# First batch of an attention and feed-forward kernel: float32 kept through the second mixing and the product with v

## Chip, cores and metric

The kernel runs on one core of one Trainium2 chip. The metric is the device time of one execution in microseconds (us). The engines are named as in the profile: PE (matmul), PEld (its weight loads), DVE (vector), ACT (scalar, activation), POOL (GpSimd), SP (the queue that issues the transfers). Each engine works through its own queue in order.

## What is computed

Four batches, 12 heads, 448 rows, head size 64, all float32 inputs. The attention mixes the 12 heads twice, once before and once after the softmax; the result goes through a feed-forward network of width 2048 with a gate.

```python
scores = scale * np.matmul(q, k.transpose(0, 1, 3, 2))
scores = np.einsum('bhij,hg->bgij', scores, w_pre)
scores = scores - np.max(scores, axis=-1, keepdims=True)
attn = np.exp(scores)
attn = attn / (np.sum(attn, axis=-1, keepdims=True) + 1e-09)
attn = np.einsum('bhij,hg->bgij', attn, w_post)
out = np.matmul(attn, v)
# then, with x = out as (1792, 768):
h = x @ w_in
g = h * (1.0 / (1.0 + np.exp(-1.702 * h)))
y = g @ w_out
```

## The kernel before

**Tiling.** A batch's 448 rows are cut into 45 groups of 10 rows (the last has 8). A group with its 12 heads makes 120 partitions, and a mixing over heads is one matmul with a 120x120 matrix that holds the 12x12 weights once for each row. Twelve groups make a chunk of 120 rows; a batch has four chunks. Four batches of 45 groups are 180 steps, and the main loop (L895 to L965) issues the work of one step after the other.

**One group's way.** `gather` (L263) brings the scores of the group from DRAM. `mix` (L273, PE, float32) applies the first mixing. `peak` (L282, DVE) takes the negative maximum, `expo` (L288) the exponential and its sum on ACT, and a small POOL instruction (L297) adds 1e-9 to the sum. `inverse` (L300, DVE) is the reciprocal. Then the weights are normalized and cut into two float16 parts: `weigh` (L304, POOL) and `upper` (L312, ACT) both multiply by the reciprocal, `lower` (L318, POOL) takes the difference. `post` (L326, PE) is the second mixing, transposed: four column blocks of 112, each with three float16 products (upper by upper, upper by lower, lower by upper: L334 to L336). `keep_upper` (L348, ACT) and `keep_lower` (L352, DVE) bring its result out of PSUM, again as two float16 parts. `context` (L358, PE) multiplies them with v, which is also kept as two float16 parts, made for batch 0 by three ACT or POOL instructions (L192, L196) and three DVE instructions (L200). `x_upper` and `x_lower` (L383, L387) take the result out.

**What is issued in a step.** At step i: `gather(i+4)`, `mix(i+1)`, `keep_upper(i-4)`, `weigh`, `upper` and `lower` of group i-1, `peak(i)`, `expo(i)`, then the jobs of the planner, `post(i-3)`, scores and contexts that are due, `keep_lower(i-4)` and, last, `inverse(i)`. PSUM holds two result tiles of the second mixing (`pp`, bufs=2).

**The planner.** `job` and `run_jobs` (L650, L656) hold work that is not tied to a group: the sums of squares and scales of q, k and v, and the conversion of 16 weight blocks from 64-bit to two float16 parts (`convert`, L422), each with 15 DVE instructions for the bits (L442 to L462), 3 for the lower part (L495), 3 sums of squares on ACT (L96) and 3 upper parts on ACT or POOL (L490, L492). Each engine has a budget of tokens (`spend`, `refill`) of 4.3 per step, never above 4.5; a job that isn't urgent waits until its engine has half its cost. `add_all` (L104) sums over partitions with a small matmul (L108) into the last 16 columns of the last `pp` tile, and DVE reads it (L109).

**After the first batch.** When a batch's attention is done, its feed-forward units are put between the steps (`hidden`, `project`, L545 and L584, on PE), 2.15 quanta to a step; after the last step only they remain.

Of the kernel before, what the change touches and what calls it, by code (L numbers as in the profile page):

```python
# [9 lines left out]
F32 = mybir.dt.float32  # L10
# [3 lines left out]
AF = mybir.ActivationFunctionType  # L14
# [8 lines left out]
GI = 10  # L23
# [15 lines left out]
def attention_then_feed_forward(ctx, tc, q, k, v, w_pre, w_post, w_in, w_out, out):  # L39
# [76 lines left out]
    def load(name, b, i, use, tag="op"):  # L116

        t = st[name, b, i] = flow.tile(SH[name], F32, name=f"{name}{use}{i}_{b}", tag=tag, bufs=THIRDS)
        w = t.shape[1]
        nc.sync.dma_start(out=t, in_=SRC[name][b][:, i * w:(i + 1) * w])  # L120

    def load_whole(name, i):

        t = st[name, 0, i] = flow.tile(
            [128, NPAIR // THIRDS, S], F32, name=f"{name}f{i}_0", tag=f"{name}p{i}"
        )
        w = t.shape[1]
        nc.sync.dma_start(out=t, in_=SRC[name][0][:, i * w:(i + 1) * w])

# [17 lines left out]
    def scale(name, b):  # L147

        m = top_of(name, b)
        e = stat.tile([128, 1], F32, name=f"e{name}_{b}", tag="e" + name)  # L150
        s = stat.tile([128, 1], F32, name=f"s_{name}{b}", tag="s" + name)
        root_bits(e, m)
        nc.vector.reciprocal(s, e)
        nc.vector.tensor_scalar_mul(s, s, 2.0 ** -50)
        nc.vector.tensor_scalar_mul(e, e, 2.0 ** 63)
        st["e" + name, b], st["s" + name, b] = e, s
        if name == "v":
            nc.vector.tensor_scalar(
                ex[:, b:b + 1], e, e_wp, 2.0 ** -12, op0=ALU.mult, op1=ALU.mult
            )  # L160

    def mixing(b):
        wa = keep.tile([KG, KG], F32, name=f"wa_{b}", tag="wa", bufs=2)
# [34 lines left out]
    def lower_part(name, b, i, eng="D"):  # L198
        u, l, src, s = pair_of(name, b, i)
        nc.vector.scalar_tensor_tensor(l, src, s, u, op0=ALU.mult, op1=ALU.subtract)  # L200
# [59 lines left out]
    def rows_of(g):  # L260
        return g * GI, min(GI, S - g * GI)
# [26 lines left out]
    def expo(i):  # L288
        K = rows_of(steps[i][1])[1] * H
        e = flow.tile([KG, S], F32, name=f"e_{i}", tag="e", bufs=3)  # L290
        sm = stat.tile([KG, 1], F32, name=f"sm_{i}", tag="sm")
        nc.scalar.activation(  # L292
            e[:K], row.pop(("mx", i))[:K, :S], AF.Exp, bias=row.pop(("nm", i))[:K, 0:1],
            scale=1.0, accum_out=sm[:K, 0:1],
        )
        rs = stat.tile([KG, 1], F32, name=f"rs_{i}", tag="rs")
        nc.gpsimd.tensor_scalar(rs[:K], sm[:K], 1e-9, 2.0 ** -10, op0=ALU.add, op1=ALU.mult)  # L297
        row["e", i], row["rs", i] = e, rs

    def inverse(i):  # L300
        K = rows_of(steps[i][1])[1] * H
        nc.vector.reciprocal(row["rs", i][:K], row["rs", i][:K])  # L302

    def weigh(i):  # L304
        K = rows_of(steps[i][1])[1] * H
# [34 lines left out]
    def mixed_to(i, j):  # L340
# [4 lines left out]
            st["p", b, c, j] = mixed.tile([CP, NR, H, CI], F16, name=f"p{j}_{b}_{c}", tag=f"p{j}")  # L345
        return st["p", b, c, j].rearrange("p r h i -> p (r h) i")[:, :, off:off + n]

    def keep_upper(i):  # L348
        row["p1", i] = mixed_to(i, 1)
        nc.scalar.copy(row["p1", i], row["pp", i])  # L350
# [7 lines left out]
    def context(b, c, pr):  # L358
        i0, n = chunk(b, c)
        if pr % 3 == 0:  # L360
            av = bank(f"av_{b}_{c}_{pr}", "av", 1)
            st["av"] = av[:, :3 * n].rearrange("p (a i) -> p a i", i=n)
        av = st["av"]
        terms = [(jc, i, j) for jc in range(NR) for i, j in ((0, 1), (0, 2), (1, 1))]
        w = H // THIRDS
        for t, (jc, i, j) in enumerate(terms):
            for d in range(2):
                h = 2 * pr + d
                nc.tensor.matmul(  # L369
                    av[d * D:(d + 1) * D, pr % 3, :],  # L370
                    st["vp", b, h // w][:, i, h % w, jc * D:(jc + 1) * D],
                    st["p", b, c, j][:, jc, h, :n],
                    start=(t == 0), stop=(t == len(terms) - 1),
                )
        return av

    def x_of(b):
        if ("x", b) not in st:
            st["x", b] = flow.tile([128, 2, NCC, S], F16, name=f"x_{b}", tag="x", bufs=2)
            st["mx", b] = stat.tile([128, 2 * NCH], F32, name=f"mx_{b}", tag="mxs", bufs=2)  # L380
        return st["x", b]

    def x_upper(b, c, half, av):  # L383
        i0, n = chunk(b, c)
        nc.scalar.activation(x_of(b)[:, 0, 3 * half:3 * half + 3, i0:i0 + n], av, AF.Copy, scale=2.0 ** -15)

    def x_lower(b, c, half, av):  # L387
        i0, n = chunk(b, c)
        x = x_of(b)[:, :, 3 * half:3 * half + 3, i0:i0 + n]
        nc.vector.scalar_tensor_tensor(  # L390
            x[:, 1], av, 2.0 ** -15, x[:, 0], op0=ALU.mult, op1=ALU.subtract
        )

    def x_size(b, c, half):
# [228 lines left out]
    def spend(eng, cost):  # L623
        tokens[eng] -= cost
# [25 lines left out]
    def job(first, eng, cost, f, after=(), stage=None, urgent=False):  # L650
        j = {"urgent": urgent, "first": first, "eng": eng, "cost": cost, "f": f, "stage": stage,
             "after": [a if isinstance(a, tuple) else (a, 1) for a in after]}
        jobs.append(j)
        return j
# [175 lines left out]
    for i in range(AHEAD):  # L830
        gather(i)
    for i in range(THIRDS):
        load("v", 0, i, "a")
    sq = []
    for i in range(THIRDS):
        stage_users["op"].append([])
        sq.append(job(1, {"A": 1.6}, 0, lambda eng, i=i: squares("v", 0, i, eng, 2), urgent=True))
    j = job(1, "D", 0.2, lambda: join("v", 0), after=sq, urgent=True)
    j = job(1, "D", 0.7, lambda: scale("v", 0), after=[j], urgent=True)
    for i in range(THIRDS):  # L840
        up = job(1, {"A": 1.0, "G": 1.6}, 0, lambda eng, i=i: upper_part("v", 0, i, eng), after=[j], urgent=True)
        low = job(1, "D", 1.05, lambda i=i: lower_part("v", 0, i), after=[up], urgent=True)
        stage_users["op"][i] += [sq[i], up, low]


    at_scores = {}
# [48 lines left out]
    while quanta or i < N + LAG + 12:  # L895
        dense = i >= N + LAG
        t_step = 4.3 if not x_done else 5.2
        refill(t_step)
        if i + AHEAD < N:
            b, g = steps[i + AHEAD]  # L900
            assert (b, g // GPC) == (0, 0) or (b, g // GPC, NPAIR - 1) in sent
            gather(i + AHEAD)
        fetch_ahead(i)
        if i + 1 < N:
            mix(i + 1)
        if 0 <= i - LAG - 1 < N:
            keep_upper(i - LAG - 1)
            spend("A", 0.55)
        if 0 <= i - 1 < N:
            weigh(i - 1)  # L910
            spend("G", 0.87)
            upper(i - 1)
            spend("A", 0.6)
            lower(i - 1)
            spend("G", 1.07)
        if i < N:
            peak(i)
            spend("D", 0.62)
            expo(i)
            spend("A", 0.82)  # L920
        run_jobs(i)
        slot()
        if x_done:
            owed += RATE
        if owed >= 1 and do_quantum(i):
            owed -= 1
            slot()
        if 0 <= i - LAG < N:
            post(i - LAG)
        for b, c, pr in at_scores.pop(i, []):  # L930
            while quanta and quanta[0][0] == "h" and quanta[0][3]:
                do_quantum(i)
                owed -= 1
            start(scores_chain(b, c, pr, *scores(b, c, pr)))
        for b, c, pr in at_context.pop(i, []):
            if c == 0 and pr == 0 and b >= 2:
                while h_done.get(NS * (b - 1) - 1, 0) < 6:
                    assert do_quantum(i)
                    slot()
            av = context(b, c, pr)  # L940
            if pr % 3 == 2:
                start(context_chain(b, c, pr, av))
            if c == NCH - 1 and pr == NPAIR - 1:
                z = i
                a = job(z + 2, "D", 0.2, lambda b=b: join_x(b), urgent=True)

                def finish(b=b, z=z):
                    scale_x(b)
                    x_done[b] = cur[0] + 1
                job(z + 3, "D", 0.9, finish, after=[a], urgent=True)  # L950
        slot()
        while owed >= 1 and do_quantum(i):
            owed -= 1
            slot()
        if 0 <= i - LAG - 1 < N:
            keep_lower(i - LAG - 1)
            spend("D", 0.64)
        if i < N:
            inverse(i)
            spend("D", 0.15)  # L960
        owed = min(owed, 3.0)
        if i >= N + LAG + 8:
            owed += 3
        cur = [i + 1]
        i += 1  # L965
# [40 lines left out]
```

## Time and profile before

| what | value |
|---|---|
| median of 3 runs | 1103.3 us (1103.12 to 1106.03) |
| profiled execution | 1107.87 us, of which the span of instructions is 1106.1 us |
| busy share of the span | PE 86%, DVE 63%, ACT 57%, POOL 41% |
| mean granted clock of PE | 0.907 |

The profiled execution is 4.6 us above the median. Its span is cut here at 37 us (first mixing), 251 us (the exponential of group 44, the last of batch 0), 300 us, 500 us and 950 us (last group of batch 3). Busy shares are averages over stages; what ends last in a stage is read from the chain of waits in that stage.

### The profile page before, as it was taken

What the parts mean: (1) busy time and instruction counts of PE and PEld (TensorE: products, weight loads), DVE (VectorE), ACT (ScalarE), POOL (GpSimd) and SP (SyncE); (2) the same over time, 40 slices, a digit from 0 to 9 for tenths busy, and PEclk for the clock granted to TensorE, in tenths of its full rate; (3) what the DMA queues carried; (4) which work ended last, traced back from release to release, by engine and by line L of the source; (5) the groups of instructions that cost most, each with busy time, mean ns of one, the idle gap of its engine ahead of it and who ended that gap; (6) DMA issues with size and microseconds to landing.
All of it is one profiled execution on the core that took longest, in us unless ns stands there. A gap on an engine that the chain in (4) does not pass through costs nothing.

```text
span 1106.1 us, 20863 instructions
## 1 busy us (share of the span) xinstructions
PE 948.5 (86%) x7716; PEld 545.1 (49%) x7716; DVE 699.2 (63%) x1455; ACT 631.3 (57%) x1432; POOL 452.9 (41%) x612
## 2 busy tenths in 40 slices
PE   3577676778688897689979899999999999999998
PEld 1233434445445554346546555565555566555554
DVE  4489777968887859956565357554664556543334
ACT  2466676676666665566565756755655555422332
POOL 0254546645553435545454345434443444210221
PEclk7577868877788899899999999999999999999999
DMA  7776776586576766655476654654654532234332
GB/s 250 212 244 225 264 269 203 158 282 192 178 226 212 242 202 207 208 168 186 130 212 211 204 174 154 204 185 134 205 168 142 179 105 88 75 120 144 114 114 79
DMA packets 67433, 201.00 MB, mean 182 GB/s; under 512 B 7764, under 2 KB 32468, under 8 KB 67332
## 3 DMA queue, kind: packets, MB, share of 16 engines
q1 hardware_dynamic: 66928, 199.59, 56.7%
q8 instruction: 61, 1.00, 0.4%
q14 instruction: 40, 0.33, 0.1%
q10 hardware_dynamic: 404, 0.09, 0.1%
HBM read 143.02 MB, written 56.62 MB: 180 GB/s over the span
## 4 chain that ended last, share of the span: by engine, by line
PE 56%; DVE 26%; ACT 7%; issue 5%; DMA 4%; POOL 1%; SPq 1%; ACTq 0%; DVEq 0%; POOLq 0%
PE po L584 18%; PE h L545 17%; PE mx L278 7%; PE av L369 4%; DVE w_p L495 3%; DVE p L353 3%; PE qk L242 3%; DVE nm L285 2%; DVE w_f L442 2%; PE pp L334 2%; DVE w_f L456 2%; DVE w_f L446 2%; PE pp L335 2%; PE pp L336 2%; DVE w_f L462 2%
## 5 line engine op out<-in xcount | busy, mean ns | idle before, releaser
L321 POOL TENSOR_TENSOR a<-w,a 120x448 f16<-120x448 f32 x180 | 201.2, 1118 | 153.0 <-issue 85.9
L584 PE MATMUL po<-g,wt 128*128 128x448 f16 x1152 | 250.7, 362 | 11.2 <-DVE th L566 7.2
L545 PE MATMUL h<-x,wt 128*128 128x448 f16 x1152 | 245.1, 357 | 3.3 <-ACT pt L608 1.7
L307 POOL TENSOR_SCALAR w<-e,rs 120x448 f32<-120x448 f32 x180 | 122.2, 679 | 306.7 <-DVE rs L302 281.8
L278 PE MATMUL mx<-r,wa 120*120 120x448 f32 x360 | 195.3, 628 | 29.0 <-DMA r<-sd 19.3
L315 ACT ACTIVATE a<-e,rs 120x448 f16<-120x448 f32 x180 | 121.4, 674 | 159.9 <-DVE rs L302 159.8
L334 PE MATMUL pp<-wp,a 120*112 120x120 f16 x720 | 140.0, 232 | 54.9 <-DVE p L353 54.4
L584 PEld LDWEIGHTS <-wt 128*128 128x128 f16 x1152 | 111.0, 100 | 135.3 <-issue 52.9
L545 PEld LDWEIGHTS <-wt 128*128 128x128 f16 x1152 | 109.5, 99 | 114.0 <-issue 28.8
L614 DVE SCALAR_TENSOR_TENSOR acc<-po,ct,acc 128x448 f32<-128x448 f32 x137 | 93.3, 682 | 81.1 <-PE po L584 79.1
L336 PE MATMUL pp<-wp,a 120*112 120x120 f16 x720 | 139.2, 231 | 0.0
L335 PE MATMUL pp<-wp,a 120*112 120x120 f16 x720 | 139.2, 231 | 0.0
L335 PEld LDWEIGHTS <-a 120*112 120x112 f16 x720 | 103.4, 144 | 56.7 <-issue 50.6
L334 PEld LDWEIGHTS <-a 120*112 120x112 f16 x720 | 103.1, 143 | 53.9 <-DVE p L353 31.8
L566 DVE SCALAR_TENSOR_TENSOR th<-th,h 128x448 f32<-128x448 f32 x64 | 39.7, 620 | 134.2 <-ACT th L563 134.2
L563 ACT ACTIVATE th<-h,ct 128x448 f32<-128x448 f32 x64 | 40.5, 633 | 146.4 <-PE h L545 129.9
L292 ACT ACTIVATE e<-mx,nm 120x448 f32<-120x448 f32 x180 | 112.7, 626 | 14.4 <-DVE nm L285 14.2
L353 DVE TENSOR_TENSOR p<-pp,p 112x480 f16<-112x480 f32 x180 | 116.3, 647 | 4.1 <-ACT p L350 4.1
L285 DVE TENSOR_REDUCE nm<-mx 120x1 f32<-120x448 f32 x180 | 108.8, 605 | 14.1 <-PE mx L278 14.1
L252 ACT COPY sc<-qk 120x448 f32<-120x448 f32 (+1 forms) x186 | 89.6, 532 | 48.4 <-PE qk L232 21.1
L350 ACT CAST p<-pp 112x480 f16<-112x480 f32 x180 | 101.3, 563 | 15.4 <-PE pp L336 15.4
L336 PEld LDWEIGHTS <-a 120*112 120x112 f16 x720 | 103.7, 144 | 0.0
(120 smaller groups left out, 1167.2 us busy)
## 6 DMA issues: line engine op xcount, KB each, us to landing
wt<-wd SPq DMA_DIRECT2D x64, 768.0 KB, 5.2
r<-sd SPq DMA_DIRECT2D x176, 210.0 KB, 3.9
sd<-sc SPq DMA_DIRECT2D x72, 420.0 KB, 6.3
w<-in_moe_w_in_dram SPq DMA_DIRECT2D x24, 512.0 KB, 4.3
w<-in_moe_w_out_dram SPq DMA_DIRECT2D x24, 512.0 KB, 6.2
wd<-w_p SPq DMA_DIRECT2D x16, 768.0 KB, 5.8
sd<-sc SPq DMA_DIRECT2D x24, 308.0 KB
va<-in_v_dram SPq DMA_DIRECT2D x12, 448.0 KB, 6.7
```

The costliest lines, as they stand in the source:

```text
L278: nc.tensor.matmul(mx[:K, :S], st["wa", b][:K, :K], row.pop(("r", i))[:K, :], start=True, stop=True)
L285: nc.vector.tensor_reduce(nm[:K], row["mx", i][:K, :S], axis=AX.X, op=ALU.max, negate=True)
L292: nc.scalar.activation(e[:K], row.pop(("mx", i))[:K, :S], AF.Exp, bias=row.pop(("nm", i))[:K, 0:1], scale=1.0, accum_out=sm[:K, 0:1],)
L307: nc.gpsimd.tensor_scalar(w[:K], e[:K], row["rs", i][:K, 0:1], 1.0, op0=ALU.mult, op1=ALU.mult)
L315: nc.scalar.activation(a1[:K], row.pop(("e", i))[:K], AF.Copy, scale=row.pop(("rs", i))[:K, 0:1])
L321: nc.gpsimd.tensor_tensor(a2[:K], row.pop(("w", i))[:K], row["a1", i][:K], op=ALU.subtract)
L334: nc.tensor.matmul(o, a1[:K, js], wp1[:K, :, :n], start=True, stop=False)
L335: nc.tensor.matmul(o, a1[:K, js], wp2[:K, :, :n], start=False, stop=False)
L336: nc.tensor.matmul(o, a2[:K, js], wp1[:K, :, :n], start=False, stop=True)
L353: nc.vector.tensor_tensor(mixed_to(i, 2), row.pop(("pp", i)), row.pop(("p1", i)), op=ALU.subtract)
L545: nc.tensor.matmul(h, w[:, i, c, fc * 128:(fc + 1) * 128], x[:, j, c, :], start=(n == 0), stop=(n == len(terms) - 1),)
L584: nc.tensor.matmul(po, w[:, j, fc, e * 128:(e + 1) * 128], g[:, i, fc, :], start=(n == 0), stop=(n == len(terms) - 1),)
```

## The change

It concerns batch 0 alone. The exponentials stay float32 and unnormalized: `weigh`, `upper` and `lower` of its 45 groups go, and POOL instead multiplies the 120x120 second mixing matrix by the reciprocal (`weigh_mix`). The second mixing is then four float32 matmuls (`post_whole`) in place of twelve float16 ones, its result is copied out of PSUM once, in two halves (`keep_whole`), the first on ACT, the second on DVE or ACT by the tokens, and the product with v is eight float32 matmuls for two heads in place of 24 float16 ones. v of batch 0 is loaded whole and not cut; its scale goes as a reciprocal into `x_upper` and `x_lower`. The second mixing is issued one step earlier relative to its group and ahead of the step's jobs, and its result is read at the head of the next step.

```diff
 def scale(name, b):
+            if b == 0:
+                xs = st["xs"] = keep.tile([128, 1], F32, name="xs")
+                nc.vector.reciprocal(xs, ex[:, 0:1])
...
+    def weigh_mix(i):
+        K = rows_of(steps[i][1])[1] * H
+        t = row["wr", i] = flow.tile([KG, H, GI], F32, name=f"wr_{i}", tag="a1", bufs=3)
+        nc.gpsimd.tensor_scalar(
+            t[:K], wp[:K], row.pop(("rs", i))[:K, 0:1], 1.0, op0=ALU.mult, op1=ALU.mult
+        )
+    def post_whole(i):
...
+        for jc in range(NR):
+            nc.tensor.matmul(
+                pp[:CP, jc * K:(jc + 1) * K], e[:K, jc * CP:(jc + 1) * CP], wr[:K, :, :n],
+                start=True, stop=True,
+            )
+        last_pp.append(pp)
...
+    def keep_whole(i):
...
+        w = NR // 2
+        for x in range(2):
...
+            src = pp[:, x * w * H:(x + 1) * w * H, :]
+            if x and tokens["D"] > tokens["A"]:
+                nc.vector.tensor_copy(o, src)
+                spend("D", 0.39)
+            else:
+                nc.scalar.copy(o, src)
+                spend("A", 0.32)
...
 def context(b, c, pr):
+        if b == 0:
+            for jc in range(NR):
+                for d in range(2):
+                    h = 2 * pr + d
+                    nc.tensor.matmul(
+                        av[d * D:(d + 1) * D, pr % 3, :],
+                        st["v", 0, h // w][:, h % w, jc * D:(jc + 1) * D],
+                        st["p", 0, c, jc // 2][:, jc % 2, h, :n],
+                        start=(jc == 0), stop=(jc == NR - 1),
+                    )
+            return av
...
-    for i in range(THIRDS):
-        up = job(1, {"A": 1.0, "G": 1.6}, 0, lambda eng, i=i: upper_part("v", 0, i, eng), after=[j], urgent=True)
-        low = job(1, "D", 1.05, lambda i=i: lower_part("v", 0, i), after=[up], urgent=True)
...
 main loop, step i:
         if i + 1 < N:
             mix(i + 1)
-        if 0 <= i - LAG - 1 < N:
+        if 0 <= i - 2 < GPB:
+            post_whole(i - 2)
+        if 0 <= i - 3 < GPB:
+            keep_whole(i - 3)
+        if GPB <= i - LAG - 1 < N:
             keep_upper(i - LAG - 1)
-        if 0 <= i - 1 < N:
+        if 0 <= i - 1 < GPB:
+            weigh_mix(i - 1)
+            spend("G", 0.35)
+        elif 0 <= i - 1 < N:
             weigh(i - 1)
...
-        if 0 <= i - LAG < N:
+        if GPB <= i - LAG < N:
             post(i - LAG)
...
-        if 0 <= i - LAG - 1 < N:
+        if GPB <= i - LAG - 1 < N:
             keep_lower(i - LAG - 1)
```

## Rows read from the trace of the kernel before

**Rows 1.** The page, chain that ended last, by engine, whole span.
```profile
PE 56%; DVE 26%; ACT 7%; issue 5%; DMA 4%; POOL 1%; SPq 1%; ACTq 0%; DVEq 0%; POOLq 0%
```
**Rows 2.** Stretches: start:end length, busy (count) PE PEld DVE ACT POOL, clock, DMA share, GB/s.
```profile
37.00:251.00 214.00, 153.70 (x1112) 86.58 (x1113) 174.30 (x360) 144.54 (x350) 108.16 (x146) 0.75 0.72 232
...
300.00:500.00 200.00, 165.84 (x1302) 94.47 (x1301) 158.63 (x322) 127.66 (x295) 90.47 (x115) 0.91 0.67 210
500.00:950.00 450.00, 430.36 (x3929) 256.35 (x3927) 251.17 (x537) 273.96 (x620) 201.15 (x287) 0.98 0.53 165
```
**Rows 3.** Chain by line in 37 to 251 us, shares of that stretch.
```profile
by line: issue 12.0%; DVE w_p L495 7.8%; DVE p L353 7.3%; DVE w_f L456 7.1%; DVE nm L285 5.9%; DVE w_f L446 5.8%; ACT waste L96 5.0%; DVE w_f L462 4.7%; DVE w_f L442 4.2%; PE qk L232 3.7%; DVE w_f L450 3.7%; PE mx L278 3.6%; ACT sc L252 3.1
```
**Rows 4.** Waits in 37 to 251 us: who <- whom: us, times, longest.
```profile
PE pp L334 <- DVE p L353: 31.6, 18, 2.9
...
DVE w_n L109 <- PE pp L108: 13.3, 5, 4.2
...
PE pp L108 <- ACT p L350: 12.4, 6, 3.2
...
DVE rs L302 <- POOL rs L297: 11.3, 10, 1.4
```
**Rows 5.** Groups by line and shape, 37 to 251 us: busy us, mean ns | idle before.
```profile
L321 POOL TENSOR_TENSOR a<-w,a 120x448 f16<-120x448 f32 x43 | 48.5, 1128 | 29.4 <-issue 12.1 <-ACT a L315 10.7 <-POOL w L307 6.3
...
L353 DVE TENSOR_TENSOR p<-pp,p 112x480 f16<-112x480 f32 x41 | 26.6, 649 | 0.7 <-ACT p L350 0.7
...
L456 DVE SCALAR_TENSOR_TENSOR w_f<-w,w_f 128x512 int32<-128x512 int32 x23 | 20.7, 899 | 0.6
L495 DVE SCALAR_TENSOR_TENSOR w_p<-w_f,w_s,w_p 128x512 f16<-128x512 f32 x21 | 20.5, 1024 | 0.0
...
L446 DVE TENSOR_SCALAR w_f<-w_f 128x512 f32<-128x512 f32 x23 | 16.3, 710 | 0.6
...
L200 DVE SCALAR_TENSOR_TENSOR vp<-va,s_v,vp 112x1024 f16<-112x1024 f32 x3 | 3.7, 1279 | 0.0
...
L390 DVE SCALAR_TENSOR_TENSOR x<-av,x 128x360 f16<-128x360 f32 x5 | 2.6, 521 | 0.0
```
**Rows 6.** Three lines of the conversion, same stretch: ns min/median/max, first and last start.
```profile
L446 DVE TENSOR_SCALAR w_f<-w_f x23: 426/428/1256, 43.2 to 231.2; 128x512 f32<-128x512 f32 x23
...
L456 DVE SCALAR_TENSOR_TENSOR w_f<-w,w_f x23: 679/831/1437, 44.1 to 236.7; 128x512 int32<-128x512 int32 x23
...
L495 DVE SCALAR_TENSOR_TENSOR w_p<-w_f,w_s,w_p x21: 737/831/1522, 48.4 to 220.8; 128x512 f16<-128x512 f32 x21
```
**Rows 7.** Timeline of a step without conversion work: start us, us, instruction.
```profile
134.51 1.03 POOL L321 TENSOR_TENSOR a<-w,a 120x448 f16<-120x448 f32 x1 [0.16 <-POOL w L307]
134.80 0.19 ACT L292 ACTIVATION_READ_ACCUMULATOR e<-mx,nm 120x1 f32 x1
...
135.64 0.19 POOL L297 TENSOR_SCALAR rs<-sm 120x1 f32<-120x1 f32 x1
```
**Rows 8.** Timeline of PE at 2.4 and 1.2 GHz: mixings and products with v.
```profile
121.11 0.82 PE L369 MATMUL av<-p,vp 112*64 112x120 f16 x24
...
121.86 1.01 PE L278 MATMUL mx<-r,wa 120*120 120x448 f32 x2
...
124.53 0.21 PE L334 MATMUL pp<-wp,a 120*112 120x120 f16 x1 [1.66 <-DVE p L353]
...
125.11 0.22 PE L336 MATMUL pp<-wp,a 120*112 120x120 f16 x1
...
133.03 1.41 PE L369 MATMUL av<-p,vp 112*64 112x120 f16 x24 [2.43 <-DVE x L390]
...
134.38 1.85 PE L278 MATMUL mx<-r,wa 120*120 120x448 f32 x2
```
**Rows 9.** Two neighbouring stretches, columns as in the first stretches above.
```profile
105.00:113.00 8.00, 7.51 (x35) 4.18 (x34) 6.74 (x15) 5.24 (x13) 4.28 (x6) 0.58 0.84 278
113.00:120.00 7.00, 4.19 (x53) 2.59 (x54) 5.44 (x18) 3.56 (x8) 2.44 (x4) 1.00 0.97 348
```

More of the change, by code (lines that the diff above doesn't have):

```diff
@@ L122, in load_whole @@
     def load_whole(name, i):
-        t = st[name, 0, i] = flow.tile(
-            [128, NPAIR // THIRDS, S], F32, name=f"{name}f{i}_0", tag=f"{name}p{i}"
-        )
+        t = st[name, 0, i] = flow.tile(SH[name], F32, name=f"{name}f{i}_0", tag=f"{name}p{i}")
         w = t.shape[1]
@@ L296, in expo @@
         rs = stat.tile([KG, 1], F32, name=f"rs_{i}", tag="rs")
-        nc.gpsimd.tensor_scalar(rs[:K], sm[:K], 1e-9, 2.0 ** -10, op0=ALU.add, op1=ALU.mult)
+        by = 2.0 ** -10 if steps[i][0] else 1.0
+        nc.gpsimd.tensor_scalar(rs[:K], sm[:K], 1e-9, by, op0=ALU.add, op1=ALU.mult)
         row["e", i], row["rs", i] = e, rs
@@ L302, in inverse @@
         nc.vector.reciprocal(row["rs", i][:K], row["rs", i][:K])
+    def weigh_mix(i):
[5 more added lines that the diff above has]
+    def post_whole(i):
+        n = rows_of(steps[i][1])[1]
+        K = n * H
+        e, wr = row.pop(("e", i)), row.pop(("wr", i))
+        pp = ps.tile([128, 512], F32, name=f"pp_{i}", tag="pp", bufs=2)
+        for jc in range(NR):
[4 more added lines that the diff above has]
+        last_pp.append(pp)
+        row["pp", i] = pp[:CP, :NR * K].rearrange("p (x i) -> p x i", i=n)
     def weigh(i):
@@ L346, in mixed_to @@
         return st["p", b, c, j].rearrange("p r h i -> p (r h) i")[:, :, off:off + n]
+    def keep_whole(i):
+        b, g = steps[i]
+        n = rows_of(g)[1]
+        c, off = g // GPC, (g % GPC) * GI
+        pp = row.pop(("pp", i))
+        w = NR // 2
+        for x in range(2):
+            if off == 0:
+                st["p", b, c, x] = mixed.tile([CP, w, H, CI], F32, name=f"pf{x}_{b}_{c}", tag=f"p{x + 1}")
+            o = st["p", b, c, x].rearrange("p r h i -> p (r h) i")[:, :, off:off + n]
+            src = pp[:, x * w * H:(x + 1) * w * H, :]
[5 more added lines that the diff above has]
+                spend("A", 0.32)
     def keep_upper(i):
@@ L363, in context @@
         av = st["av"]
+        w = H // THIRDS
+        if b == 0:
[9 more added lines that the diff above has]
+            return av
         terms = [(jc, i, j) for jc in range(NR) for i, j in ((0, 1), (0, 2), (1, 1))]
-        w = H // THIRDS
         for t, (jc, i, j) in enumerate(terms):
@@ L384, in x_upper @@
         i0, n = chunk(b, c)
-        nc.scalar.activation(x_of(b)[:, 0, 3 * half:3 * half + 3, i0:i0 + n], av, AF.Copy, scale=2.0 ** -15)
+        by = st["xs"] if b == 0 else 2.0 ** -15
+        nc.scalar.activation(x_of(b)[:, 0, 3 * half:3 * half + 3, i0:i0 + n], av, AF.Copy, scale=by)
     def x_lower(b, c, half, av):
@@ L389, in x_lower @@
         x = x_of(b)[:, :, 3 * half:3 * half + 3, i0:i0 + n]
+        by = st["xs"] if b == 0 else 2.0 ** -15
         nc.vector.scalar_tensor_tensor(
-            x[:, 1], av, 2.0 ** -15, x[:, 0], op0=ALU.mult, op1=ALU.subtract
+            x[:, 1], av, by, x[:, 0], op0=ALU.mult, op1=ALU.subtract
         )
@@ L832, in attention_then_feed_forward @@
     for i in range(THIRDS):
-        load("v", 0, i, "a")
-    sq = []
-    for i in range(THIRDS):
-        stage_users["op"].append([])
-        sq.append(job(1, {"A": 1.6}, 0, lambda eng, i=i: squares("v", 0, i, eng, 2), urgent=True))
-    j = job(1, "D", 0.2, lambda: join("v", 0), after=sq, urgent=True)
-    j = job(1, "D", 0.7, lambda: scale("v", 0), after=[j], urgent=True)
-    for i in range(THIRDS):
-        up = job(1, {"A": 1.0, "G": 1.6}, 0, lambda eng, i=i: upper_part("v", 0, i, eng), after=[j], urgent=True)
-        low = job(1, "D", 1.05, lambda i=i: lower_part("v", 0, i), after=[up], urgent=True)
-        stage_users["op"][i] += [sq[i], up, low]
+        load_whole("v", i)
+    sq = [job(1, {"A": 1.6}, 0, lambda eng, i=i: squares("v", 0, i, eng, 2), urgent=True) for i in range(THIRDS)]
+    j = job(1, "D", 0.2, lambda: join("v", 0), after=sq, urgent=True)
+    job(1, "D", 0.9, lambda: scale("v", 0), after=[j], urgent=True)
     at_scores = {}
```

## Prediction

> **What bounds the kernel now.** I read the chain of waits of the whole span first: PE holds 56% of it and DVE 26% [rows 1]. Then the stretches [rows 2], since the change touches batch 0 alone. From 500 to 950 us PE is busy 430 of 450 us; nothing of that stage is changed, so it can only start earlier or later. From 37 to 251 us, where the 45 groups of batch 0 are mixed, DVE is the busiest engine, 174.3 of 214 us, and PE 153.7 at a mean granted clock of 0.75, that is now at 1.2 and now at 2.4 GHz. The chain of that stretch alone [rows 3] shows who ends last: the six DVE lines of the weight conversion make 33.3% of it (7.8 + 7.1 + 5.8 + 4.7 + 4.2 + 3.7), the lower part of the second mixing on DVE (L353) 7.3%, the peak 5.9%; PE's lines that can be seen make 3.7 and 3.6%. So the first 250 us are paced by DVE, with PE waiting on it: the second mixing waited 31.6 us for L353, which frees its PSUM tile at the end of DVE's step [rows 4]. From 300 to 500 us DVE and PE are both near 80% busy [rows 2]. What batch 0 saves should therefore be carried to the end: the loop issues by step, and each later step keeps its work, apart from conversion jobs that freed tokens may bring forward.
>
> **The change part by part.** Times are made against the profiled execution, 1107.9 us; the median is 4.6 us lower, and I subtract the same change from it.
>
> (a) *L353 goes.* It took 649 ns, 41 times in the stretch [rows 5]. Its share of the chain is 7.3% of 214 = 15.6 us, against 26.6 us busy; in steps without conversion work it lies beside the wait for the exponential. For all 45 groups: 15.6 x 45/41 = -17 us. Bounds: 0 where PE takes over, -29 (45 x 0.649) if all of it counted.
>
> (b) *The three lower parts of v go*, 3.7 us of DVE in one step [rows 5], urgent and in front of that step's L353: -3.7 us. Their upper parts are on ACT and POOL, beside DVE: nothing. One more reciprocal on one column costs DVE nothing that can be seen in the sum.
>
> (c) *POOL's big instructions go.* L446 took 426 ns at the least but 710 in the mean, L456 679 and 899, L495 737 and 1024 [rows 5, 6]: 23 x 0.284 + 23 x 0.220 + 21 x 0.287 = 17.6 us of stretching. What POOL does beside them is for the largest part L321, 48.5 of its 108.2 busy us [rows 2, 5], 45%. Taking that share of the excess gives 7.9 us; of the three lines' 57.5 us, 20.7% of 214 = 44.3 us lie on the chain, 77%: -6 us. Bounds 0 and -17.6. The new instruction on POOL works on 120 columns where L321 had 448. The Trainium skill ("SBUF — State Buffer", Who interferes with whom) says that VectorE and GpSimd share a port pair as an exclusive lock, so that one that comes second waits for the whole of the other's instruction. The trace agrees that the longest L446 (1256 ns) is nearly three times the shortest. By that page every GpSimd instruction that reads memory counts alike, L307 too; were all of the 17.6 us to go, (c) would be 17.6 x 0.77 = 13.6 us, an estimate, in place of 6.
>
> (d) *A half copy is added on DVE* where its tokens exceed ACT's. No row shows 240 columns; 480 columns took 649 ns and 360 took 521 [rows 5], which is 1.07 ns a column, so about 0.39 us. The planner may choose DVE in few or all groups, 15 to 45; I take 30, since DVE spends less per step than before and its budget is often at the cap: 11.7 us, at L353's share on the chain (15.6 of 26.6) +7 us. Bounds +3.5 and +17.6. It stands at the head of DVE's step and waits for the second mixing of the step before; the peak and the conversion are queued behind it.
>
> (e) *The reciprocal comes sooner in light steps.* There POOL's L321 runs until 135.54 and only then the small L297, though the sum of the exponentials was read at 134.99 [rows 7]; DVE waited 11.3 us in 10 such places for L297 [rows 4]. Up to 0.6 us each is lost to L321. The copy of (d) takes part of it: -4 us; bounds 0 and -6.
>
> (f) *The small sums of the planner.* Their matmul writes into the last `pp` tile. Before, ACT had just been given that tile's copy, so PE waited 12.4 us for it (6 times), and DVE 13.3 us for PE (5 times) [rows 4]. Now the last tile is the one just written, whose readers come a step later. The sum must still be ready on ACT; I take half: -6 us; bounds 0 and -13.
>
> (g) *PE has more to do.* A float32 mixing of 448 columns takes 1.01 us at 2.4 GHz and 1.85 at 1.2 [rows 8]. In proportion to 120 columns, four make 1.08 and 1.98 us. The twelve float16 matmuls take 0.80 us at 2.4 GHz (124.53 to 125.33), and by the ratio of the two products with v (1.41/0.82) about 1.38 at 1.2 GHz [rows 8]: +0.28 or +0.60 a group. The product with v is eight float32 matmuls, two at a time, so again 1.08 or 1.98 against 0.82 or 1.41: +0.26 or +0.57, 24 times. Over the batch 19 us at the high clock, 41 at the low, 29 at the mix of the stretch. PE is idle for 60 of 214 us [rows 2], and 31.6 us of that is the wait on L353 that goes [rows 4]; this idle time hides most of it. On the path I put a quarter, +7 us; bounds 0 and +29.
>
> (h) *At no cost:* ACT loses two instructions a group and gets one or two half copies, and no longer waits for the reciprocal; the new POOL multiplication waits for the reciprocal where `weigh` did, and its reader is a step later; SP's queue keeps the same transfers in the same order. Scales read from a column instead of a constant keep their instruction.
>
> Sum: -17 - 3.7 - 6 + 7 - 4 - 6 + 7 = -22.7 us, 1085 us for a run like the profiled one and 1080.6 against the median. I forecast 1080.
>
> **The rivals.**
>
> *PE becomes the bound of batch 0 (slower).* With 29 us more, PE has 183 us of work at the clock mix of the stretch, in a stretch that should shrink to 191: it decides when the clock falls under about 0.72. At 0.6, the 153.7 us become 192 and the addition about 35: 227 against 214, so the stage grows by 13 us and none of DVE's savings is seen: 1116. For it: at clock 0.58 PE was already busy 7.5 of 8 us [rows 9]. Against it: right behind that stretch the clock was 1.00 and PE busy only 4.2 of 7 us [rows 9]; a busier PE was answered with the high clock.
>
> *Something else is next at once (no change).* DVE's freed time is filled: with more tokens the planner puts conversion jobs into steps that were light, or transfers are late, whose engines reached a share of 0.97 [rows 9] against a mean of 0.72. Only (b) and half of (a) would be left, less (d): -12 + 7 = -5, about 1098; with PE's +7 it is 1103 or more. Against: conversion brought forward is missing from the stage up to 500 us, where DVE is 79% busy, and gathers are issued four steps ahead.
>
> *The stretching goes wholly.* (c) at -17.6 and (a) at -25 give -42: 1061. For it: L321 is what POOL does most. Against: the upper parts of the conversion stay on POOL, and the planner may send it more of them.
>
> **How the numbers follow.** Forecast 0.65, the larger gain 0.10, nothing gained 0.11, PE as the bound 0.14. A measurement of this kernel can tell about 0.3%, 3.3 us, from no change; the "no change" case reaches to both sides of that. Faster 0.77, same 0.09, slower 0.14. The range takes in the larger gain and the edge of "no change": 1057 to 1105; the bounds of (a) to (g) added all together would reach further on both sides, but they exclude each other in part, as more PE on the path goes with less of DVE.
>
> **What would show it.** Right, if L353 is gone before 251 us, the means of L446, L456 and L495 there come near their least, the second mixing no longer waits for DVE, the exponential of group 44 comes some 20 to 25 us earlier, and everything after 500 us looks as before, shifted. Step (g) is wrong if a float32 second mixing takes far more than 1.1 us at 2.4 GHz, or if PE's lines take DVE's place in the chain of batch 0. The forecast fails if the granted clock of the stretch falls, or if the 45 steps shorten but the stage up to 500 us gives it back.

## The result and the profile after

| kernel | median us (runs) | ratio to the kernel before, 95% interval |
|---|---|---|
| before | 1103.2 (1098.8 to 1106.0) | 1 |
| changed | 1083.4 (1081.6 to 1086.8) | 0.984, 0.981 to 0.986 |
| changed, measured again beside e9 | 1081.6 (1079.6 to 1083.2) | 0.981, 0.977 to 0.984 |

The change made the kernel faster by 1.6 to 1.9%, some 20 us; 1080 had been forecast. The profiled execution after took 1085.2 us with a span of 1083.4 us, 22.7 us less than the one before.

Where the time went is read from the same places as before. The exponential of group 44 ends batch 0's chain of groups; it stood at 251 us and now starts at 234.16 us:

```profile
234.16 0.63 ACT L293 ACTIVATE e<-mx,nm 96x448 f32<-96x448 f32 x1 [1.55 <-DVE nm L286]
```

So 17 us came in batch 0. At group 60 the lead was 16 us, at group 90 22 us, and from there it stayed at 22 to 23 us to the end: some 6 us more came between 300 and 500 us. That less conversion work was left there fits, but no run tests it. Line numbers have moved: L495 to L515 are now the bits of the conversion (L442 to L462 before), L548 its lower part (L495), L286 the peak, L293 the exponential, L319 the float32 second mixing, L385 and L382 the two half copies on ACT and DVE.

Stretches of the changed kernel, with the columns of [rows 2]: length, busy time (count) of PE, PEld, DVE, ACT, POOL, granted clock, DMA share, GB/s.

```profile
37.00:234.00 197.00, 141.49 (x820) 91.05 (x822) 145.32 (x371) 114.47 (x318) 48.25 (x107) 0.86 0.79 261
...
283.00:483.00 200.00, 169.89 (x1388) 97.79 (x1387) 155.74 (x318) 129.24 (x297) 89.85 (x116) 0.94 0.65 204
483.00:928.00 445.00, 425.94 (x3877) 253.55 (x3876) 244.95 (x524) 268.79 (x610) 195.91 (x282) 0.98 0.53 164
```

Against [rows 2], DVE in batch 0 went from 174.3 busy us of 214 to 145.3 of 197, POOL from 108 to 48, and the clock rose from 0.75 to 0.86. DVE's share fell from 81 to 74%: it is no longer as clearly the pace-maker. The chain of that stretch, to be held against [rows 3], says the same:

```profile
by line: DVE nm L286 8.3%; PE mx L279 7.2%; issue 7.1%; ACT waste L96 6.3%; DVE w_f L509 5.6%; PE pp L319 5.6%; DVE w_p L548 5.0%; DVE w_f L515 4.9%; ACT sc L253 4.0%; DMA sd<-sc 4.0%; DVE w_f L503 4.0%; PE av L409 3.8%; DMA wd<-w_p 3.7%; D
```

DVE's lines that can be seen still make the largest part, 27.8%, but PE's make 16.6%, where those seen in [rows 3] made 7.3%, and transfers 7.7%, where none could be seen. Groups by line and shape in 37 to 234 us, to be held against [rows 5]:

```profile
L319 PE MATMUL pp<-wr,e 120*112 120x120 f32 x336 | 49.2, 298 | 0.0
...
L509 DVE SCALAR_TENSOR_TENSOR w_f<-w,w_f 128x512 int32<-128x512 int32 x26 | 19.0, 731 | 0.7
...
L548 DVE SCALAR_TENSOR_TENSOR w_p<-w_f,w_s,w_p 128x512 f16<-128x512 f32 x24 | 16.5, 742 | 0.0
L309 POOL TENSOR_SCALAR wr<-wp,rs 120x120 f32<-120x120 f32 x44 | 16.1, 367 | 66.8 <-DVE rs L304 60.2 <-PE qk L233 3.7 <-PE mx L279 3.0
...
L499 DVE TENSOR_SCALAR w_f<-w_f 128x512 f32<-128x512 f32 x26 | 12.3, 472 | 0.8
L382 DVE COPY pf<-pp 112x240 f32<-112x240 f32 x30 | 12.0, 400 | 28.9 <-ACT pf L385 28.9
```

The three conversion lines are 731, 742 and 472 ns in the mean, where they were 899, 1024 and 710: nearly their shortest. Three parts more of the conversion fit into a stretch that is 17 us shorter. The last row holds what was not foreseen: DVE's half copies are busy for 12 us, but DVE stood idle for 28.9 us in front of them. The waits of the same stretch (who waited for whom: us, times, longest):

```profile
PE mx L279 <- ACT e L293: 28.9, 20, 3.7
DVE pf L382 <- ACT pf L385: 28.9, 16, 5.1
...
PE pp L108 <- ACT waste L96: 8.4, 4, 3.0
...
DVE w_n L109 <- PE pp L108: 5.7, 3, 4.6
```

The second mixing's wait for DVE, 31.6 us in [rows 4], is gone. DVE's wait for the small sums fell from 13.3 to 5.7 us, and PE's wait ahead of them is now for the sum of squares itself. In their place PE's first mixing waits for the exponential, and DVE's copy waits for ACT's copy. One such place in order of time (start us, us, instruction; in brackets the idle time before it and what ended it):

```profile
215.95 0.95 ACT L253 COPY sc<-qk 120x448 f32<-120x448 f32 x2
...
216.78 0.37 ACT L385 COPY pf<-pp 112x240 f32<-112x240 f32 x1
...
217.19 0.41 DVE L382 COPY pf<-pp 112x240 f32<-112x240 f32 x1 [5.05 <-ACT pf L385]
```

ACT works through sums of squares and score copies first, then makes its half; DVE stands for 5 us with the peak and the conversion queued behind the copy, although both halves only read the tile and go to different tiles. The PSUM tile had been written long before. The Trainium skill states the rule behind it ("PSUM — Partial Sum Buffer", PSUM bank collisions raise a hardware error): two engines must not touch one bank of the same partitions at the same time, reads included, and the compiler therefore orders any two of them. The trace agrees: each of the 16 waits ends within 0.04 us of the end of ACT's half, and in none of the 32 places do the two copies overlap.

### The profile page after: what moved, and what is told of

It reads as the page before. It is cut to its first block, busy times and chain, and to the rows that moved or that the text cites. A ratio compares the mean times of both kernels' runs of the same rounds, so it can differ in the third digit from the quotient of the medians.

```text
span 1083.4 us, 20018 instructions
## 1 busy us (share of the span) xinstructions
PE 934.9 (86%) x7344; PEld 549.3 (51%) x7344; DVE 656.2 (61%) x1444; ACT 595.4 (55%) x1389; POOL 383.5 (35%) x567
## 4 chain that ended last, share of the span: by engine, by line
PE 59%; DVE 21%; ACT 8%; DMA 7%; issue 4%; SPq 0%; POOL 0%; ACTq 0%; DVEq 0%; POOLq 0%
PE po L637 18%; PE h L598 17%; PE mx L279 8%; PE av L420 4%; PE qk L243 3%; DVE nm L286 3%; DVE w_p L548 2%; PE pp L356 2%; DMA r<-sd 2%; DMA sd<-sc 2%; PE pp L358 2%; PE pp L357 2%; ACT waste L96 2%; DVE w_f L509 2%; DVE w_f L515 2%
## 5 line engine op out<-in xcount | busy, mean ns | idle before, releaser
L279 PE MATMUL mx<-r,wa 120*120 120x448 f32 x360 | 187.7, 605 | 60.6 <-ACT e L293 38.6
L343 POOL TENSOR_TENSOR a<-w,a 120x448 f16<-120x448 f32 x135 | 150.8, 1117 | 124.3 <-issue 69.4
L329 POOL TENSOR_SCALAR w<-e,rs 120x448 f32<-120x448 f32 x135 | 91.0, 674 | 239.6 <-DVE rs L304 220.4
L293 ACT ACTIVATE e<-mx,nm 120x448 f32<-120x448 f32 x180 | 113.3, 629 | 84.2 <-DVE nm L286 51.1
L337 ACT ACTIVATE a<-e,rs 120x448 f16<-120x448 f32 x135 | 91.0, 674 | 118.7 <-DVE rs L304 118.7
L667 DVE SCALAR_TENSOR_TENSOR acc<-po,ct,acc 128x448 f32<-128x448 f32 x141 | 96.0, 682 | 83.8 <-PE po L637 81.8
L286 DVE TENSOR_REDUCE nm<-mx 120x1 f32<-120x448 f32 x180 | 109.1, 606 | 13.7 <-PE mx L279 13.7
L279 PEld LDWEIGHTS mx<-r,wa 120*120 120x120 f32 x360 | 61.9, 194 | 101.9 <-ACT e L293 55.0
L356 PE MATMUL pp<-wp,a 120*112 120x120 f16 x540 | 97.3, 222 | 18.8 <-DVE p L393 18.2
L299 POOL TENSOR_SCALAR rs<-sm 120x1 f32<-120x1 f32 x180 | 56.5, 314 | 134.2 <-ACT e L293 122.2
L358 PE MATMUL pp<-wp,a 120*112 120x120 f16 x540 | 96.7, 221 | 0.0
L357 PE MATMUL pp<-wp,a 120*112 120x120 f16 x540 | 96.5, 220 | 0.0
L393 DVE TENSOR_TENSOR p<-pp,p 112x480 f16<-112x480 f32 x135 | 87.1, 646 | 3.0 <-ACT p L390 2.9
L356 PEld LDWEIGHTS <-a 120*112 120x112 f16 x540 | 72.5, 134 | 27.4 <-DVE p L393 13.3
L357 PEld LDWEIGHTS <-a 120*112 120x112 f16 x540 | 72.8, 135 | 19.8 <-issue 13.6
```

The costliest lines, as they stand in the source:

```text
L279: nc.tensor.matmul(mx[:K, :S], st["wa", b][:K, :K], row.pop(("r", i))[:K, :], start=True, stop=True)
L286: nc.vector.tensor_reduce(nm[:K], row["mx", i][:K, :S], axis=AX.X, op=ALU.max, negate=True)
L293: nc.scalar.activation(e[:K], row.pop(("mx", i))[:K, :S], AF.Exp, bias=row.pop(("nm", i))[:K, 0:1], scale=1.0, accum_out=sm[:K, 0:1],)
L329: nc.gpsimd.tensor_scalar(w[:K], e[:K], row["rs", i][:K, 0:1], 1.0, op0=ALU.mult, op1=ALU.mult)
L337: nc.scalar.activation(a1[:K], row.pop(("e", i))[:K], AF.Copy, scale=row.pop(("rs", i))[:K, 0:1])
L343: nc.gpsimd.tensor_tensor(a2[:K], row.pop(("w", i))[:K], row["a1", i][:K], op=ALU.subtract)
```

## The experiments

Each is the changed kernel (for e8 the kernel of e1) with one thing altered, measured beside the kernel before on the same chip. Differences are worked out from the ratios to the kernel before, times 1103.2 us, against 1083.6 us, which is the mean of the changed kernel's two ratios (0.9822). These two lie 3 us apart, and the changed kernel was not run beside e1 to e8, so a difference of 3 us says nothing.

| experiment | median us | ratio, interval | against the changed kernel |
|---|---|---|---|
| e1 both copies on ACT | 1066.8 | 0.967, 0.963 to 0.971 | -17 |
| e2 DVE's copy at the step's end | 1071.8 | 0.972, 0.969 to 0.976 | -11 |
| e3 POOL's lower part back | 1092.4 | 0.992, 0.989 to 0.995 | +11 |
| e4 DVE's lower part back | 1100.7 | 0.998, 0.996 to 1.000 | +17 |
| e5 second mixing twice | 1087.8 | 0.986, 0.980 to 0.992 | +4.5 |
| e6 second mixing behind the jobs | 1093.5 | 0.991, 0.988 to 0.995 | +10 |
| e7 ACT's upper part back | 1084.1 | 0.983, 0.980 to 0.986 | +1 |
| e8 e1, copies behind the exponential | 1066.3 | 0.967, 0.964 to 0.970 | -17 |
| e9 DVE copies first | 1068.6 | 0.969, 0.965 to 0.973 | -14 |

The first four tell apart DVE's work, POOL's stretching and the new wait.

**e1, both copies on ACT.**

```diff
-            if x and tokens["D"] > tokens["A"]:
-                nc.vector.tensor_copy(o, src)
-                spend("D", 0.39)
-            else:
-                nc.scalar.copy(o, src)
-                spend("A", 0.32)
+            nc.scalar.copy(o, src)
+            spend("A", 0.32)
```

> The changed kernel with both half copies of the second mixing's result on ACT. In the changed kernel's trace DVE's half (L382) starts only when ACT's half (L385) has ended, though both only read the tile: 33 us of DVE waiting in 17 places up to 240 us, which the prediction didn't have. Theory 1 (this wait is on the path): without it the kernel gets 8 to 15 us faster than the changed one, about 1070 us, and group 44's exponential comes before 226 us instead of 234. Theory 2 (DVE's wait is slack; ACT is what DVE would wait for anyway, through the exponential and the peak): within 3 us of the changed kernel, about 1083, and the wait turns up at another DVE line. Theory 3 (ACT has no room for 32 more half copies): slower by up to 10 us, 1093.

Measured: 17 us faster than the changed kernel, a little more than theory 1's 8 to 15, and 3.3% faster than the kernel before. DVE's wait was on the path. The stretch of batch 0 in e1, same columns as above:

```profile
37.00:221.00 184.00, 137.71 (x829) 88.04 (x830) 135.23 (x341) 121.53 (x351) 50.70 (x107) 0.87 0.83 277
```

Group 44 comes at 220.6 us, 13.5 us earlier than in the changed kernel. ACT is busy for 121.5 of 184 us, so it had the room, and theory 3 falls.

**e2, DVE's half at the end of the step.**

```diff
-                nc.vector.tensor_copy(o, src)
+                row["late", i] = (o, src)
...
+        if ("late", i - 3) in row:
+            nc.vector.tensor_copy(*row.pop(("late", i - 3)))
         if i < N:
             inverse(i)
```

> The changed kernel with DVE's half copy issued at the end of the step, ahead of the reciprocal, instead of at its head; where the planner chooses DVE is unchanged. By then ACT's half is long done. Theory 1 (the wait at the head is on the path): 8 to 15 us faster than the changed kernel, like e1. Theory 2 (slack): within 3 us. Against it: the PSUM tile is freed later, at the end of DVE's step as in the kernel before; if that matters, the second mixing waits for DVE again and up to 8 us are lost.

Measured: 11 us faster. Same work on DVE, only behind the conversion instead of ahead of it. So the wait at the head was worth at least 11 us, since e2 also pays for a tile that is freed later. The other 6 us between e2 and e1 may be that and the DVE work itself; no run separates them, and the two intervals overlap. That the second mixing waits for DVE again shows in e2's list of 37 to 234 us:

```profile
PE pp L319 <- DVE rs L304: 19.3, 12, 4.6
```

**e3, POOL's lower part back.**

```diff
             weigh_mix(i - 1)
             spend("G", 0.35)
+            a2 = flow.tile([KG, S], F16, name=f"again_{i}", tag="again")
+            K = rows_of(steps[i - 1][1])[1] * H
+            e = row["e", i - 1]
+            nc.gpsimd.tensor_tensor(a2[:K], e[:K], e[:K], op=ALU.subtract)
```

> The changed kernel with one POOL instruction per group of batch 0 put back: two inputs of 120x448 float32, output float16, as the old lower part (1.1 us), its result unused. Theory of the prediction, terms (c) and (e): DVE's conversion lines are stretched again and the sum's small POOL instruction comes late, so the kernel is 6 to 14 us slower than the changed one, 1089 to 1097, and the means of the conversion lines in batch 0 rise by 100 to 300 ns. Rival (the stretching costs nothing, since DVE has slack now): within 3 us of the changed kernel although the means rise.

Measured: 11 us slower, inside the forecast. Groups of e3 in 37 to 234 us:

```profile
L965 POOL TENSOR_TENSOR again<-e 120x448 f16<-120x448 f32 x42 | 43.6, 1037 | 0.0
L548 DVE SCALAR_TENSOR_TENSOR w_p<-w_f,w_s,w_p 128x512 f16<-128x512 f32 x24 | 20.4, 901 | 0.0
...
L509 DVE SCALAR_TENSOR_TENSOR w_f<-w,w_f 128x512 int32<-128x512 int32 x24 | 18.2, 757 | 0.7
...
L499 DVE TENSOR_SCALAR w_f<-w_f 128x512 f32<-128x512 f32 x25 | 13.3, 530 | 0.8
```

An unused POOL instruction lengthens DVE instructions that don't depend on it: 742 to 901 ns, 731 to 757, 472 to 530. The rise was expected at 100 to 300 ns and is that large in one of the three lines only. But other DVE lines are stretched too. From 37 us to the exponential of group 44, with the same 371 instructions, DVE is busy for 155.96 us in e3 (second line) against 145.38 in the changed kernel (first line):

```profile
37.00:234.16 197.16, 141.65 (x821) 91.21 (x823) 145.38 (x371) 114.47 (x318) 48.25 (x107) 0.85 0.79 261
```
```profile
37.00:242.19 205.19, 147.47 (x821) 93.11 (x823) 155.96 (x371) 114.33 (x318) 92.83 (x151) 0.82 0.77 251
```

That is 10.6 us, about what e3 costs. The late reciprocal (term e) has little part in it: up to 234 us DVE's wait for the small POOL instruction (L299) is 6.8 us in the changed kernel, 7.7 in e3 and was 11.3 in [rows 4].

**e4, DVE's lower part back.**

```diff
+        if 0 <= i - 3 < GPB:
+            pp = row.pop(("pp", i - 3))
...
+            z = wp1[:CP, :, :n].unsqueeze(1).to_broadcast([CP, NR, H, n])
+            t = flow.tile([CP, NR, H, GI], F16, name=f"again_{i}", tag="again")
+            nc.vector.tensor_tensor(t[:, :, :, :n], pp, z, op=ALU.subtract)
         if i < N:
             inverse(i)
```

> The changed kernel with one DVE instruction per group of batch 0 put back at the end of the step, of the old lower part's kind and size (112x480 from PSUM, a float16 input, float16 output, result unused); it holds the PSUM tile to the end of DVE's step as the old one did. Term (a): 17 us slower than the changed kernel, about 1100, with bounds of 0 (PE or ACT sets the pace now) and 29 us (all 45 x 0.65 us count). Rival (DVE no longer sets the pace): under 5 us slower.

Measured: 17 us slower, as term (a) said; nearly the whole gain is gone. Like L353, the added instruction both works on DVE and holds the PSUM tile, and the 17 us are the price of the two together. The same 37 to 234 us in e4, where batch 0 lasts longer, and the wait that came back:

```profile
37.00:234.00 197.00, 147.58 (x745) 86.90 (x746) 154.44 (x375) 109.00 (x300) 47.01 (x101) 0.79 0.75 244
```
```profile
PE pp L319 <- DVE rs L304: 29.9, 17, 3.0
```

DVE is busy for 154 of 197 us instead of 145, the second mixing waits 29.9 us for the end of DVE's step (31.6 in [rows 4]), and the clock falls from 0.86 to 0.79.

The next three price the terms that the prediction had put at a quarter, a half and nothing.

**e5, PE's second mixing twice.**

```diff
-        for jc in range(NR):
+        for jc in [*range(NR)] * 2:
             nc.tensor.matmul(
                 pp[:CP, jc * K:(jc + 1) * K], e[:K, jc * CP:(jc + 1) * CP], wr[:K, :, :n],
```

> The changed kernel with the four float32 matmuls of batch 0's second mixing issued twice (the second time over the first, same result). In the changed kernel's trace eight records of one such mixing take 0.98 us at 2.4 GHz and 1.72 at 1.2, so PE gets 40 to 70 us more work over 45 groups. Term (g) of the prediction put a quarter of PE's added time on the path: 10 to 17 us slower than the changed kernel, 1093 to 1100. Rival 1 (PE's idle time hides it, and a busier PE holds the high clock): under 5 us slower, granted clock of the batch above 0.86. Rival 2 (PE sets the pace of batch 0 by now): 30 us or more slower.

Measured: 4.5 us slower, with an interval of about 6.7 us to either side. That is rival 1, not to be told from nothing; the lower end of term (g)'s 10 to 17 us lies just inside the interval. Batch 0 in e5:

```profile
37.00:234.00 197.00, 165.84 (x1154) 120.18 (x1156) 145.08 (x371) 114.79 (x318) 49.44 (x107) 0.92 0.80 262
```

PE is busy for 166 of 197 us instead of 141, and its clock is granted at 0.92 instead of 0.86. PE's idle time takes most of the added work; rival 2 falls clearly.

**e6, the second mixing behind the jobs.**

```diff
-        if 0 <= i - 2 < GPB:
-            post_whole(i - 2)
         if 0 <= i - 3 < GPB:
             keep_whole(i - 3)
...
+        if 0 <= i - 2 < GPB:
+            post_whole(i - 2)
         if GPB <= i - LAG < N:
             post(i - LAG)
```

> The changed kernel with the second mixing issued behind the step's jobs, as in the kernel before, instead of ahead of them. The planner's small sums then write into the tile that ACT is about to copy, and PE and DVE wait for that copy again. Term (f): 6 us slower than the changed kernel, about 1089 (bounds 0 and 13), with the wait of L108 on ACT's copy back in the list. Rival: no difference (within 3 us), the small sums then wait for something else for as long, the sum of squares on ACT.

Measured: 10 us slower. So half of the gain hangs on the place of one call. In e6's list of waits for 37 to 234 us the small sums wait for the copy of the tile that they write into, now the one on DVE:

```profile
DVE pf L382 <- ACT pf L385: 38.5, 18, 5.0
...
PE pp L108 <- DVE pf L382: 20.1, 9, 5.2
```

DVE's wait for ACT's half grew as well, from 28.9 us to 38.5, so the 10 us are the price of both and not of term (f) alone.

**e7, ACT's upper part back.**

```diff
+            rs = row["rs", i - 1]
             weigh_mix(i - 1)
             spend("G", 0.35)
+            a1 = flow.tile([KG, S], F16, name=f"again_{i}", tag="again")
+            K = rows_of(steps[i - 1][1])[1] * H
+            nc.scalar.activation(a1[:K], row["e", i - 1][:K], AF.Copy, scale=rs[:K, 0:1])
```

> The changed kernel with one ACT instruction per group of batch 0 put back ahead of the exponential: the old upper part, 120x448 float32 times the reciprocal into float16, result unused. It holds ACT's queue until DVE has issued the reciprocal of the group before. Term (h) of the prediction priced ACT's relief at nothing: then within 3 us of the changed kernel, 1083. Rival (ACT's queue is on the path, since the copies and the exponential stand behind that wait): 10 to 25 us slower.

Measured: 1 us slower, no difference. ACT does 0.67 us more per group and waits for the reciprocal again:

```profile
ACT again L965 <- DVE rs L304: 31.6, 23, 3.8
```

That wait of 31.6 us costs nothing, while DVE's of 28.9 us in the changed kernel cost 11 to 17: the sum of a wait says nothing without the engine's place on the path.

**e8, the copies behind the exponential.**

```diff
 e1, and:
-        if 0 <= i - 3 < GPB:
-            keep_whole(i - 3)
...
             expo(i)
             spend("A", 0.82)
+        if 0 <= i - 3 < GPB:
+            keep_whole(i - 3)
```

> The kernel of e1 (both half copies on ACT) with the copies issued behind the step's exponential instead of ahead of it. In e1's trace PE's first mixing waits for the exponential, which frees its PSUM tile, 21 us on the matmuls and 36 on the weight loads up to 225 us. If the two copies (0.74 us) ahead of the exponential lengthen that ring: 5 to 10 us faster than e1 (1067), about 1060. If transfers set the pace of e1 by now (DMA share 0.83 in batch 0): within 3 us of e1.

Measured: the same as e1. So the place of the copies ahead of the exponential costs e1 nothing. PE's wait for the exponential itself stayed (on the matmuls from 37 to 234 us 20.6 us in e1, 22.9 in e8), so whether that wait holds e1 is not tested. That transfers do fits: the DMA share is 0.83 in batch 0 of e1, against 0.72 in [rows 2], and e1's chain from 37 to 225 us has three transfer lines of 4 to 6% that can be seen. No run changes a transfer, so it is not shown.

```profile
by line: issue 8.1%; PE mx L279 7.1%; DMA ka<-in_k_dram 5.8%; DMA sd<-sc 5.2%; DVE w_f L505 4.8%; DVE nm L286 4.7%; ACT waste L96 4.6%; PE pp L319 4.4%; PE qk L233 4.2%; DMA wd<-w_p 4.2%; DVE w_f L511 3.9%; DVE w_p L544 3.8%; DMA w<-in_moe_
```

**e9, DVE copies first.**

```diff
-            if x and tokens["D"] > tokens["A"]:
+            if x == 0:
+                on_dve = tokens["D"] > tokens["A"] - 0.32
+            if x == 0 and on_dve:
                 nc.vector.tensor_copy(o, src)
```

> The changed kernel with the halves swapped: where the planner picks DVE, DVE copies the first half and ACT the second, still at the head of the step. If the program orders the two readers of one PSUM tile in the order of issue, the wait moves: DVE's copy no longer waits for ACT, and ACT's waits for DVE. Theory 1 (the price of the half copy was DVE's wait; ACT has room, as e7 showed): 10 to 17 us faster than the changed kernel, 1066 to 1073, the 0.4 us of DVE work per copy being the rest. Theory 2 (any order between the two couples the queues and costs the same): within 4 us of 1083, the wait being ACT's now.

Measured: 14 us faster, with as much copying on DVE, 32 half copies in both. In 37 to 234 us of e9:

```profile
ACT pf L387 <- DVE pf L384: 25.3, 15, 3.9
...
DVE pf L384 <- PE pp L319: 3.8, 2, 3.2
```

The wait is nearly as long as before, but it is ACT's now, and ACT has room. So the order of the two readers follows the order of issue, and the cost depends on which engine is the second.

**The changed kernel again**, beside e9, as the base of the table.

> The changed kernel as it is, beside e9 on the same chip: 1083, the ratio to the kernel before 0.981 to 0.986. It is the base against which e1 to e9 are read.

Measured: 1081.6 us, ratio 0.981, at the lower edge of what was expected.

## Why the prediction was right

The forecast was 1080 with a range of 1057 to 1105; the kernel took 1083.4 and 1081.6 us. The sum of -22.7 us is against a measured change of about -20 us in the medians, -22.7 us in the profiled executions. But the size agrees better than the terms do, and that is partly luck: step (d) cost 10 us more than forecast, so other terms must have saved about as much more. Of the signs that the prediction named, L353 is gone, the conversion lines are near their least, the second mixing no longer waits for DVE and the clock rose; group 44 came 17 us earlier, not 20 to 25, and some 6 us more came up to 500 us.

| term | forecast us | shown by | us |
|---|---|---|---|
| (a) L353 goes | -17 | e4 | -17 |
| (b) lower parts of v | -3.7 | not run alone | - |
| (c) and (e) POOL's big instructions | -10 | e3, one of two instructions | -11 |
| (d) half copy on DVE | +7 | e1 | +17 |
| (f) small sums | -6 | e6, with DVE's longer wait | -10 |
| (g) more work on PE | +7 | e5, second mixing only | +4.5, between -2 and +11 |
| (h) ACT relieved | 0 | e7 | -1 |

The right column can't be added up as a test of the sum: its rows cover more or less than their terms, as marked, (b) was not run alone, and each is uncertain by 3 to 7 us.

*The reading of the bound was right.* DVE set the pace of batch 0; an instruction of 0.65 us put back at the same place costs 17 us (e4), as its share of the chain in [rows 3] had given, and not the 29 us that all 45 would make. The share of the chain was the better price, not the busy time.

*The stretching of step (c) was right in place and kind, and taken too small.* The three conversion lines stood 17.6 us above their shortest times, and by the means above about 3 us are left; (c) had let 7.9 us go, L321's share of POOL's work. The stand-in for L321 in e3 brings about 6 us of the three lines back. POOL's other big instruction, the multiplication by the reciprocal (L307), went too; that it did the rest of the stretching fits, but no run puts it back. So the condition of the third rival, that the stretching goes wholly, was nearly met, while its gain did not come. In the later batches, where POOL has its old work, L548 is stretched still, from 234 us to the end:

```profile
L548 DVE SCALAR_TENSOR_TENSOR w_p<-w_f,w_s,w_p 128x512 f16<-128x512 f32 x24 | 20.7, 917 | 0.0
```

The other two lines are not, or hardly: 713 ns for L509 and 501 for L499 there.

*Step (d) failed in size.* It priced DVE's copy by its duration, 0.39 us, and took the count at 30. Both were right: 32 copies of 0.41 us in the median. It named the wait for the second mixing at the head of DVE's step, and left out that the copy also waits for ACT's half of the same PSUM tile, and with it for all that ACT has in front of it. The price of the term is 17 us (e1), of which at least 11 are that wait (e2), where the upper bound had been 17.6. The rule that would have said so is the one of the Trainium skill cited above ("PSUM — Partial Sum Buffer", PSUM bank collisions raise a hardware error); the row for ACT's and DVE's copies of one tile was missing in the trace before, since there DVE needed ACT's result anyway.

*Step (g) was sized well; its share on the path stays open.* Times at 2.4 and 1.2 GHz in the changed kernel:

```profile
126.24 0.98 PE L319 MATMUL pp<-wr,e 120*112 120x120 f32 x8
127.15 1.04 PE L409 MATMUL av<-pf,vf 112*64 112x120 f32 x16
...
217.92 1.87 PE L409 MATMUL av<-pf,vf 112*64 112x120 f32 x16
...
221.36 1.72 PE L319 MATMUL pp<-wr,e 120*112 120x120 f32 x8
```

The forecast was 1.08 and 1.98 for both. Whether a quarter of the added time was on the path is not decided: e5 adds 24 us of busy PE, of which a quarter is 6, and costs 4.5, between -2 and +11. With the wait on L353 gone, PE ran at 0.86 of the full clock instead of 0.75 and was busy for 141 of 197 us instead of 154 of 214, with more to do; in e4, with such a wait back, the clock was 0.79. PE's part of the chain grew, but it did not take DVE's place.

*The rivals.* PE as the bound needed a clock under 0.72; it rose, and e5 shows room to spare. That something else is next at once was partly so: the new wait took at least 11 us of the gain, and transfers, which this rival named, have a part of the chain that they had not before.

## What to carry to other kernels

Price an instruction that goes by its line's share of the chain in its own stage, and look also at what it does to its neighbours: here one POOL instruction a group cost 11 us by lengthening another engine's instructions, and one call's place in the step 10 us through waits on shared tiles. When a copy out of PSUM is split between two engines, the second one, as here, waits for the first and for what that has queued ahead; give the second place to the engine that has room, or give it both halves. That alone, e1, takes the kernel to 1066.8 us, 3.3% below where it began.

## What the hardware showed that was not expected

Two engines that read different columns of one PSUM tile are put one after the other: 28.9 us of waiting in 16 places on DVE in the changed kernel, 25.3 us in 15 places on ACT when the order is turned round (e9). And more work went with a faster PE: with the second mixing issued twice, the granted clock of 37 to 234 us went from 0.86 to 0.92, and 24 us more of busy PE cost 4.5 us, not told from nothing.
